# Four-unit stores, a longer scan ring and new queue orders in a fused scan and mixture-of-adapters kernel

## The chip, the core and the metric

The kernel runs on one core of a Trainium2 chip. The core has a matrix engine (PE, TensorE), a vector engine (DVE), a scalar engine (ACT), GpSimd (POOL) and a sync engine (SP). Sixteen DMA engines move data between the chip's main memory (HBM) and the core's on-chip memory; a queue of a sequencer (here mostly SP's) hands them their work. PE writes its results to eight banks of PSUM, from where ACT or DVE copy them out.

The metric is the device time of one execution in microseconds, lower is better: 201.49 us, the median of four runs (201.17 to 202.0).

## What is computed

A linear recurrence along the sequence, then a mixture of eight rank-16 adapters with the best two of eight experts for each row. Cut from the reference:

```python
# a, b: (8, 6400, 128) float32
for t in range(S):
    h = a[:, t] * h + b[:, t]
    out[:, t] = h

x = out.reshape(51200, 128)
logits = x @ w_gate                      # (51200, 8)
topk = the two largest of each row
w = softmax over the two chosen logits
delta = sum over both of  w * ((x @ A[e]) @ B[e])     # A: (8, 128, 16), B: (8, 16, 128)
return x + delta
```

26.2 MB each of a and b are read and 26.2 MB are written.

## The kernel before

**Units.** The 51,200 rows are cut into 100 units of 512 rows. A unit is one PSUM bank wide once transposed: 128 features on the partitions, 512 time steps along the row.

**The stages of a unit w**, with the names that the planner gives them:

- `lda`, `ldb` (function `load`): SP loads two units of a and two of b at a time, 512 KB each, in rows of 4 KB (one partition's share). They land in rings `a_in` and `b_in` of 8 slots, so 16 units deep (`ring`). The first a, the first two b and the last a are loaded alone, 256 KB in rows of 2 KB.
- `AB` (`transposes`): PE transposes a and b into two PSUM banks.
- `aev` (`a_evac`, L686): ACT copies the transposed a to `a_st`.
- `scan` (L710): DVE runs the recurrence and writes `xT`, a ring of `XR` = 20 units in f16.
- `ZL` (`products`): PE multiplies blocks of `xT` by the gate and all adapters' A side by side; `zl` (L767) parks the result on the chip, ACT again.
- gating (`m1`, `p1`, `r1`, `p3`, `m2`, `p4`, `r2`, `p6`, `p7`, `sig`): for groups of up to three units, on DVE, POOL and ACT. Groups among the first or last few (`quick`) take a shorter way through a MAX8 instruction on DVE.
- `mul` (L926): POOL, or DVE for some, multiplies by the gates. `T` transposes on PE, `tev` (L942) copies the result to `zwT` on DVE or ACT.
- `D` (`delta`): PE adds x (by the identity) and the product with B in a PSUM bank; `oev` (L978) copies it to `outt`, a ring of `NOUT` = 24 units.
- `st` (`store`): SP stores two units at a time, 512 KB.

**Which rows of x a partition holds.** A store wants long rows in memory. `x_block(v, q)` therefore picks columns of `xT` with a stride: for a pair of units (p, i) is split with i = 8, so that a partition gets 8 neighbouring rows of 128 floats, 4 KB, over the two units' places in `outt`. A unit that stands alone (`SOLO`) has i = 4, rows of 2 KB. Since a pair's rows are mixed over both units, products and deltas of a unit wait for the scan of the pair's last unit (`scanned`).

**Order.** Nothing is dispatched at run time: `_Plan.schedule` simulates all engines once, when the program is built, with the costs written in the code (a load of two units 1290 ns, and so on), and fixes each engine's list. Among operations that could start at the same time the one with the smaller key (unit plus the offset of its kind in `CFG["key"]`) goes first. `_Plan.run` (L243) then writes out each list; before an instruction it waits for the semaphores of what it needs (L248), and what follows on that engine waits too.

**Stores.** Store j of units from u0 has the rank u0 + `HOLD` among SP's work and waits for the evictions of its units and for the scan of unit u0 + `HOLD` (at most 99). `oev` of unit v waits for the store that last read its place, that of v - 24. All loads and stores are issued by SP in one list, by the line L429 of the helper `add_dma`; the three constants (w_gate, A, B) by ACT with the same helper at the start. A reaches `spread` (L533) on POOL and DVE, a gather on PE, and then the weights for `ZL`.

```python
        stores = [(u, 2) for u in range(0, NU - 2, 2)] + [(NU - 2, 1), (NU - 1, 1)]
...
                [f"oev{v}" for v in range(u0, u0 + n)] + [f"scan{min(u0 + HOLD, NU - 1)}"],
```

Of the kernel before, what the change touches and what calls it, by code (L numbers as in the profile page):

```python
# [11 lines left out]

CFG = {
    "ring": 8,
    "xr": 20,
    "zr": 48,
    "nout": 24,
    "hold": 20,
    "heads": (1, 1, 1, 1),
    "group": 3,  # L20
    "tails": (2, 2, 1, 1),
    "quick": (2, 2),
    "split": (4, 4),
    "solo": (2, 2),
    "mul": (0, 1, 0, 8),
    "tev": (1, 1, 4, 4),
    "tail": 8,
    "heat": 6,
    "filler": (2, 1, 1),
    "caps": {'a': 3, 'b': 4, 'Z': 1, 'O': 3, 'w': 8},  # L30
    "least": {'Z': 1, 'O': 1},
    "pairs": (98, 2),
    "ast": 3,
    "tevns": (264.0, 330.0),
    "key": {
        "AB": 170.4, "aev": 138.5, "scan": 13.3, "ZL": 157.0, "zl": 152.0, "gate": 31.6, "r1": -64.5, "r2": -65.8,
        "sig": 83.8, "mul": 73.7, "T": 119.3, "tev": 143.8, "D": 171.1, "oev": 151.4, "R": 65.1,
    },
}

# [239 lines left out]
def bass_associative_scan_2x2__then__mixture_of_adapters_kernel(  # L280
# [8 lines left out]
    NB, S, D = a.shape  # L289
    E = moe_w_gate.shape[1]  # L290
    R = moe_A.shape[2]
# [4 lines left out]
    Q = 4  # L296
    UT = 64 * QI
    assert UT == 128 * Q and N % (2 * UT) == 0 and S >= UT
    NU = N // UT
    RING = CFG["ring"]  # L300
    XR = CFG["xr"]
    NOUT = CFG["nout"]
# [33 lines left out]
    GB = GM * Q  # L336
    SOLO = [v for v in range(NU) if v < CFG["solo"][0] or v >= NU - CFG["solo"][1]]
    assert CFG["solo"][0] % 2 == 0 and CFG["solo"][1] % 2 == 0 and XR % 2 == 0 and NOUT % 2 == 0
    p0, p1 = CFG["pairs"]
    PAIRED = {w: (w - p0) % 2 for w in range(p0, NU - p1)}  # L340
    assert (NU - p0 - p1) % 2 == 0 and p0 >= 2 and p1 >= 1
# [15 lines left out]
    fills_of = {}  # L357
# [11 lines left out]
    with ExitStack() as stack:  # L369
# [4 lines left out]
        cst_f = sb(nc.sbuf_tensor("cst_f", [128, E + 256], F32))  # L374
# [14 lines left out]
        xT = sb(nc.sbuf_tensor("xT", [128, XR * UT], F16))  # L389
# [30 lines left out]
        def add_dma(name, eng, unit, starts, slot, ns, deps=(), kind="dma", issue=450.0, after=2000.0):  # L420
# [30 lines left out]
            ["id0"],  # L451
        )

        add_dma("wg_in", "act", -110, [(cst_f[:, 0:E], moe_w_gate[:, :])], ("wg",), 80.0, (), "fix", 450.0, 2000.0)
        add_dma(
            "A_in",
            "act",
            -109,
            [(cst_f[:, E : E + 128], moe_A.rearrange("e (h l) r -> (e h) (l r)", l=8))],
            ("A",),  # L460
            220.0,
# [4 lines left out]
        )  # L466
        add_dma(
            "B_in",
            "act",
            -108,  # L470
            [(cst_f[:, E + 128 : E + 256], moe_B.rearrange("e r d -> (e r) d"))],
            ("B",),
            220.0,
# [138 lines left out]
        def load(t, w):  # L612

            n = place(t, w)[0]
            many = 1 if (t, w) in alone else 2
            dst, i = rings[t][:, n % RING, :], QI
            if many == 1:
                dst, i = dst[:, column(t, w) : column(t, w) + UT], Q
            src = rows_of[t][w * UT : (w + many) * UT, :].rearrange("(p i) d -> p (i d)", i=i)
            for k in range(many):  # L620
                load_of[t, w + k] = f"ld{t}{w}"
            add_dma(
                f"ld{t}{w}",
                "sp",
                w - 2 * RING + (0 if w > 3 else -200),
                [(dst, src)],
                (t, n % RING, many, w if many == 1 else 0),
                1290.0 if many == 2 else 690.0,
                users.get((t, n - RING), []),
            )  # L630

        def transposes(w):
# [56 lines left out]
            )  # L689

        def readers(v):
            both = [v] if v in SOLO else [v - v % 2, v | 1]
            return [f"D{u}" for u in both] + [f"ZL{k}" for u in both for k in fills_of.get(u, [])]

        def scan(w):
            t0 = w * UT
# [33 lines left out]


        def x_block(v, q):
            if v in SOLO:
                x0 = (v % XR) * UT
                return xT[:, x0 : x0 + UT].rearrange("d (p i) -> d i p", i=Q)[:, q, :]
            x0 = (v - v % 2) % XR * UT
            return xT[:, x0 : x0 + 2 * UT].rearrange("d (p i) -> d i p", i=2 * Q)[:, v % 2 * Q + q, :]

        def scanned(v):
            return f"scan{v if v in SOLO else v | 1}"  # L740

        def products(k):
            b0, n = fills[k]
# [245 lines left out]
                gives=("O", v),  # L989
            )  # L990

        stores = [(u, 2) for u in range(0, NU - 2, 2)] + [(NU - 2, 1), (NU - 1, 1)]
        store_of = {v: j for j, (u0, n) in enumerate(stores) for v in range(u0, u0 + n)}

        def store(j):
            u0, n = stores[j]
            s0 = u0 % NOUT
            rows = out[u0 * UT : (u0 + n) * UT, :]
            tile, ns = outt[:, s0 : s0 + n, :], 680.0 * n
            if u0 in SOLO:  # L1000
                rows = rows.rearrange("(n p i) d -> p n (i d)", p=128, i=Q)
            else:
                rows = rows.rearrange("(p i) d -> p (i d)", p=128)
                tile, ns = tile.rearrange("p n c -> p (n c)"), 1290.0
            add_dma(
                f"st{j}",
                "sp",
                u0 + HOLD,
                [(rows, tile)],
                ("o", s0, n),  # L1010
                ns,
                [f"oev{v}" for v in range(u0, u0 + n)] + [f"scan{min(u0 + HOLD, NU - 1)}"],
            )

# [19 lines left out]
            gating(k)  # L1034
        for j in range(len(stores)):
            store(j)
        ends = [f"st{j}" for j in range(len(stores) - NOUT, len(stores))]
        add("end", "sp", "fix", 1.0e9, 10.0, lambda h: h.nop(), ends)

        plan.schedule()  # L1040
# [49 lines left out]
```

## Time and profile before

| | |
|---|---|
| median of four runs | 201.49 us (201.17 to 202.0) |
| the profiled execution | 201.28 us, of which the span from first to last instruction is 199.4 us |
| granted PE clock, mean | 0.984 |
| HBM read, written | 52.56 MB, 26.21 MB; 395 GB/s over the span |
| chain that ended last | PE 42%, DVE 20%, ACT 19%, DMA 6% |
| store of two units, issue to landing | 15.2 us (median of 49) |
| ACT copy to `a_st` | 100 copies, 61.6 us busy |
| ACT copy to `outt` | 100 copies, 61.3 us busy |
| DVE scan | 96 instructions of 128x512, 120.2 us busy |
| PE waiting for a_in or b_in | at most 2.0 us for each of the two in all |

The profile is one execution on the chip. Busy time is the union of an engine's instructions; consecutive instructions of one engine overlap, so that the mean length of one times their number is more than the busy time. PE is the matrix engine's multiplies, PEld its weight loads, which overlap them; matmuls are pipelined and their ends modelled, so a busy PE is not PE at its peak. "SPq" is SP's issuing of DMAs. A DMA queue's share is the time that its packets took, over sixteen DMA engines; packets of a queue overlap by a little, so a share can exceed 100%. A packet here is one row (2 or 4 KB) or one completion write. A line of stages reads: the window, its length, each engine's busy time and (xN) its instructions, then the granted PE clock, the DMA share and GB/s. A GB/s line has 40 equal slices of its window.

### The profile page before, as it was taken

The page shows a single profiled execution, that of the slowest core. Times are in us where ns is not written, and L with a number is a line of the kernel's source. Part 1 is how long each engine was busy: PE and PEld are TensorE (multiplying, and loading weights), DVE is VectorE, ACT ScalarE, POOL GpSimd, SP SyncE. Part 2 cuts the span into 40 slices and gives each one's busy share as a digit, 9 for nine tenths or more (in the row PEclk, how much of TensorE's full clock was granted, in tenths as well). Part 3 has the DMA queues.
Part 4 walks back from the last instruction along what each step waited for, and adds up shares of the span by engine and source line. Part 5 has one row for each costly group of instructions (what it writes and reads, how often), then busy time and mean ns, then how long its engine had stood idle before and what let it go on. Part 6 is the DMA issues. An engine that isn't in the chain of part 4 may idle for free.

```text
span 199.4 us, 8009 instructions
## 1 busy us (share of the span) xinstructions
PE 183.3 (92%) x3202; PEld 163.1 (82%) x3202; DVE 173.8 (87%) x302; ACT 179.9 (90%) x463; POOL 158.5 (80%) x278
## 2 busy tenths in 40 slices
PE   7887999999999999999999999999999999897750
PEld 4676898899999989899889998898899898795640
DVE  3799699999999999899989889889797999789940
ACT  3587899999999999999999999999999999898860
POOL 2344549889888998988799999998999989888710
PEclk9998799999999999999999999999999999999996
DMA  6999999999999999999999999999999999998993
GB/s 214 398 418 408 406 409 404 408 409 408 404 418 416 414 414 422 409 414 416 414 415 412 420 413 415 416 416 414 417 417 415 412 418 414 411 374 353 413 392 130
DMA packets 22629, 79.30 MB, mean 398 GB/s; under 512 B 2624, under 2 KB 2880, under 8 KB 22592
## 3 DMA queue, kind: packets, MB, share of 16 engines
q1 hardware_dynamic: 22160, 78.65, 98.0%
q8 instruction: 25, 0.41, 0.8%
q10 hardware_dynamic: 432, 0.14, 0.3%
q14 instruction: 12, 0.10, 0.1%
HBM read 52.56 MB, written 26.21 MB: 395 GB/s over the span
## 4 chain that ended last, share of the span: by engine, by line
PE 42%; DVE 20%; ACT 19%; DMA 6%; issue 3%; POOL 2%; SPq 2%; POOLq 1%; DVEq 0%; ACTq 0%
PE ps L94 22%; PE ps L98 20%; DVE xT L710 15%; ACT a_st L686 7%; DMA b_in<-in_b_dram 6%; ACT outt L978 5%; ACT zl L767 4%; DVE zwT L942 3%; SPq L429 2%; POOL zw L926 2%; ACT pn L816 1%; POOLq L369 1%; ACT g L905 1%; DVE zw L926 1%; POOL d L880 1%
## 5 line engine op out<-in xcount | busy, mean ns | idle before, releaser
L710 DVE TENSOR_TENSOR_SCAN xT<-a_st,xT,ps 128x512 f16<-128x512 f32 x96 | 120.2, 1252 | 10.9 <-ACT a_st L686 4.0
L926 POOL TENSOR_TENSOR zw<-zl,g 128x512 f16<-128x512 f32 x93 | 99.5, 1075 | 9.7 <-ACT g L905 8.0
L767 ACT COPY zl<-ps 128x408 f32<-128x408 f32 (+1 forms) x139 | 73.7, 537 | 1.0 <-PE ps L94 0.9
L98 PE MATMUL ps<-ident_f,a_in 64*128 64x64 f32 (+1 forms) x792 | 69.4, 231 | 1.2 <-DMA a_in<-in_a_dram 1.2
L98 PE MATMUL ps<-ident_f,b_in 64*128 64x64 f32 (+1 forms) x792 | 67.6, 230 | 1.5 <-DMA b_in<-in_b_dram 1.2
L686 ACT COPY a_st<-ps 128x512 f32<-128x512 f32 x100 | 61.6, 634 | 7.0 <-PE ps L98 6.4
L98 PEld LDWEIGHTS ps<-ident_f,a_in 64*128 64x128 f32 (+1 forms) x792 | 57.5, 140 | 8.7 <-DMA a_in<-in_a_dram 2.0
L978 ACT COPY outt<-ps 128x512 f32<-128x512 f32 x100 | 61.3, 629 | 2.2 <-PE ps L94 1.5
L98 PEld LDWEIGHTS ps<-ident_f,b_in 64*128 64x128 f32 (+1 forms) x792 | 56.5, 140 | 2.7 <-DVE m L851 1.3
L94 PE MATMUL ps<-cst_h,xT 128*128 128x136 f16 x400 | 50.7, 235 | 0.7 <-DVE xT L710 0.5
L94 PE MATMUL ps<-ident_h,xT 128*128 128x128 f16 x400 | 42.7, 229 | 1.4 <-DVE zwT L942 1.2
L98 PE MATMUL ps<-ident_h,zw 128*128 128x128 f16 x400 | 39.0, 220 | 3.7 <-DVE zw L926 2.0
L94 PEld LDWEIGHTS ps<-cst_h,xT 128*128 128x128 f16 x400 | 36.2, 148 | 4.7 <-DVE xT L710 1.4
L94 PE MATMUL ps<-cst_h,zwT 128*128 128x128 f16 x400 | 38.9, 220 | 0.0
L942 DVE COPY zwT<-ps 128x256 f32<-128x256 f32 x89 | 35.6, 408 | 2.6 <-PE ps L98 2.4
L94 PEld LDWEIGHTS ps<-ident_h,xT 128*128 128x128 f16 x400 | 33.1, 147 | 3.4 <-DVE zwT L942 2.4
L98 PEld LDWEIGHTS ps<-ident_h,zw 128*128 128x128 f16 x400 | 25.0, 98 | 7.8 <-DVE zw L926 3.0
L94 PEld LDWEIGHTS ps<-cst_h,zwT 128*128 128x128 f16 x400 | 27.4, 100 | 0.0
L816 ACT ACTIVATE pn<-d 128x96 f32<-128x96 f32 (+2 forms) x72 | 23.1, 329 | 0.8 <-POOL d L858 0.6
L866 POOL TENSOR_TENSOR L<-zl,pn 128x96 f32<-128x96 f32 (+2 forms) x34 | 13.0, 382 | 6.5 <-ACT pn L816 6.3
L888 POOL TENSOR_TENSOR d<-d 128x96 f32<-128x96 f32 (+2 forms) x36 | 13.9, 386 | 3.8 <-DVE d L841 3.3
L895 POOL TENSOR_TENSOR um<-d,pn 128x96 f32<-128x96 f32 (+2 forms) x36 | 14.3, 396 | 2.8 <-ACT pn L816 1.4
(38 smaller groups left out, 87.2 us busy)
## 6 DMA issues: line engine op xcount, KB each, us to landing
a_in<-in_a_dram SPq DMA_DIRECT2D x49, 512.0 KB, 15.4
b_in<-in_b_dram SPq DMA_DIRECT2D x49, 512.0 KB, 15.5
out_dram<-outt SPq DMA_DIRECT2D x49, 512.0 KB, 15.2
a_in<-in_a_dram SPq DMA_DIRECT2D x2, 256.0 KB, 8.9
b_in<-in_b_dram SPq DMA_DIRECT2D x2, 256.0 KB, 4.0
out_dram<-outt SPq DMA_DIRECT2D x2, 256.0 KB, 5.2
cst_f<-in_moe_A_dram ACTq DMA_DIRECT2D x1, 64.0 KB, 3.5
cst_f<-in_moe_B_dram ACTq DMA_DIRECT2D x1, 64.0 KB, 4.8
```

The costliest lines, as they stand in the source:

```text
L94: return self.handle.matmul(*args, **kwargs)
L98: return self.handle.transpose(*args, **kwargs)
L686: lambda h: h.copy(a_st[w % NAS][:, :], bank(("a", w))[:, :]),
L710: last = h.tensor_tensor_scan(out=x_at(lo, hi), data0=a_st[w % NAS][:, lo:hi], data1=bank(("b", w))[:, lo:hi], initial=init, op0=ALU.mult, ...
L767: return h.copy(zl[:, r0 : r0 + n, :], src)
L816: lambda h: h.activation(v(pn[s]), v(src[s]), ACTF.Relu, bias=bias, scale=scale),
L866: lambda h: h.tensor_tensor(out=v(L2[s]), in0=Lg, in1=v(pn[s]), op=ALU.subtract),
L888: lambda h: h.tensor_tensor(out=v(d1[s]), in0=v(d1[s]), in1=v(d2[s]), op=ALU.add),
L895: lambda h: h.tensor_tensor(out=v(um[s]), in0=v(d1[s]), in1=v(pn[s]), op=ALU.subtract),
L926: lambda h: h.tensor_tensor(out=oview, in0=zview, in1=gview, op=ALU.mult),
L942: return copy(zwT[v % NZT][:, :].bitcast(F32), bank(("O", v))[:, 0 : UT // 2])
L978: return copy(outt[:, v % NOUT, :], bank(("O", v))[:, :])
```

## The change

- Units 8 to 87 are stored four at a time, 1 MB in rows of 8 KB, the others in pairs but for the last two. `block_of` says which block a unit belongs to; `x_block`, `scanned`, `readers` and `stores` follow it. In a four-unit block the stride in `xT` is i = 16, and products and deltas wait for the scan of the block's last unit. The first two units, which stood alone, become a pair.
- The three constants are issued by POOL, A ahead of the rest.
- The `xT` ring holds 28 units rather than 20.
- A store waits for the scan 22 units on rather than 20.
- The sizes of the first and last gating groups, the number of quick groups, the split of products, the number of last units whose `mul` and `tev` may go to either of two engines, the units whose `tev` is on DVE (seven of eight rather than all between the ends), the warming multiplies at the start, the planner's costs of a load's latency and of stores, and the keys are set anew. The lists of all engines differ.
- The program's end waits for all stores rather than the last 24 of them; what that instruction waits for lies at the end of SP's list.

```diff
 CFG = {
     "ring": 8,
-    "xr": 20,
+    "xr": 28,
     "zr": 48,
     "nout": 24,
-    "hold": 20,
-    "heads": (1, 1, 1, 1),
+    "hold": 22,
+    "quads": (8, 12),
+    "heads": (1, 2, 1),
     "group": 3,
-    "tails": (2, 2, 1, 1),
-    "quick": (2, 2),
-    "split": (4, 4),
-    "solo": (2, 2),
-    "mul": (0, 1, 0, 8),
-    "tev": (1, 1, 4, 4),
-    "tail": 8,
+    "tails": (3, 2, 2),
+    "quick": (4, 2),
+    "split": (4, 8),
+    "solo": (0, 2),
+    "mul": (0, 1, 0, 10),
+    "tev": (7, 8, 4, 4),
+    "tail": 6,
     "heat": 6,
-    "filler": (2, 1, 1),
+    "filler": (2, 2, 2),
...
     "key": {
-        "AB": 170.4, "aev": 138.5, "scan": 13.3, "ZL": 157.0, "zl": 152.0, "gate": 31.6, "r1": -64.5, "r2": -65.8,
-        "sig": 83.8, "mul": 73.7, "T": 119.3, "tev": 143.8, "D": 171.1, "oev": 151.4, "R": 65.1,
+        "AB": 26.2, "aev": 28.9, "scan": 8.5, "ZL": -146.0, "zl": 94.8, "gate": -12.7, "r1": 84.9, "r2": 34.5,
+        "sig": 37.7, "mul": 31.8, "T": -42.2, "tev": 33.0, "D": 9.7, "oev": 472.4, "R": 65.09967571861861,
     },
...
+    QUAD = range(CFG["quads"][0], NU - CFG["quads"][1])
+    assert not QUAD or (XR % 4 == 0 and NOUT % 4 == 0 and QUAD[0] % 4 == 0 and len(QUAD) % 4 == 0)
+
+    def block_of(v):
+
+        n = 1 if v in SOLO else 4 if v in QUAD else 2
+        return v - v % n, n
+
...
-        add_dma("wg_in", "act", -110, [(cst_f[:, 0:E], moe_w_gate[:, :])], ("wg",), 80.0, (), "fix", 450.0, 2000.0)
+        add_dma("wg_in", "pool", -107.4, [(cst_f[:, 0:E], moe_w_gate[:, :])], ("wg",), 80.0, (), "fix", 450.0, 2000.0)
         add_dma(
             "A_in",
-            "act",
-            -109,
+            "pool",
+            -107.5,
...
         add_dma(
             "B_in",
-            "act",
-            -108,
+            "pool",
+            -107.3,
...
+                after=2000.0 if many == 2 else 1250.0,
...
         def readers(v):
-            both = [v] if v in SOLO else [v - v % 2, v | 1]
-            return [f"D{u}" for u in both] + [f"ZL{k}" for u in both for k in fills_of.get(u, [])]
+            if v < 0:
+                return []
+            u0, n = block_of(v)
+            whole = range(u0, u0 + n)
+            return [f"D{u}" for u in whole] + [f"ZL{k}" for u in whole for k in fills_of.get(u, [])]
...
         def x_block(v, q):
-            if v in SOLO:
-                x0 = (v % XR) * UT
-                return xT[:, x0 : x0 + UT].rearrange("d (p i) -> d i p", i=Q)[:, q, :]
-            x0 = (v - v % 2) % XR * UT
-            return xT[:, x0 : x0 + 2 * UT].rearrange("d (p i) -> d i p", i=2 * Q)[:, v % 2 * Q + q, :]
+            u0, n = block_of(v)
+            x0 = u0 % XR * UT
+            return xT[:, x0 : x0 + n * UT].rearrange("d (p i) -> d i p", i=n * Q)[:, (v - u0) * Q + q, :]
 
         def scanned(v):
-            return f"scan{v if v in SOLO else v | 1}"
+            u0, n = block_of(v)
+            return f"scan{u0 + n - 1}"
...
-        stores = [(u, 2) for u in range(0, NU - 2, 2)] + [(NU - 2, 1), (NU - 1, 1)]
+        stores = []
+        for v in range(NU):
+            u0, n = block_of(v)
+            if v == u0:
+                stores += [(v, n)]
...
-            rows = out[u0 * UT : (u0 + n) * UT, :]
-            tile, ns = outt[:, s0 : s0 + n, :], 680.0 * n
-            if u0 in SOLO:
-                rows = rows.rearrange("(n p i) d -> p n (i d)", p=128, i=Q)
-            else:
-                rows = rows.rearrange("(p i) d -> p (i d)", p=128)
-                tile, ns = tile.rearrange("p n c -> p (n c)"), 1290.0
             add_dma(
                 f"st{j}",
                 "sp",
                 u0 + HOLD,
-                [(rows, tile)],
+                [
+                    (
+                        out[u0 * UT : (u0 + n) * UT, :].rearrange("(p i) d -> p (i d)", p=128),
+                        outt[:, s0 : s0 + n, :].rearrange("p n c -> p (n c)"),
+                    )
+                ],
                 ("o", s0, n),
-                ns,
+                {1: 690.0, 2: 1290.0, 4: 2510.0}[n],
                 [f"oev{v}" for v in range(u0, u0 + n)] + [f"scan{min(u0 + HOLD, NU - 1)}"],
             )
...
-        ends = [f"st{j}" for j in range(len(stores) - NOUT, len(stores))]
+        ends = [f"st{j}" for j in range(len(stores))]
```

## The prediction

> **What bounds the kernel now.** I read the page first, for the engines against the DMA queues.
>
> ```profile
> span 199.4 us, 8009 instructions
> PE 183.3 (92%) x3202; PEld 163.1 (82%) x3202; DVE 173.8 (87%) x302; ACT 179.9 (90%) x463; POOL 158.5 (80%) x278
> DMA  6999999999999999999999999999999999998993
> q1 hardware_dynamic: 22160, 78.65, 98.0%
> a_in<-in_a_dram SPq DMA_DIRECT2D x49, 512.0 KB, 15.4
> ```
>
> No compute engine is full over the span, though ACT and PE come near. SP's queue q1 fills 98.0% of sixteen DMA engines' span, and a 512 KB load needs 15.4 us from issue to landing, so some twelve transfers stand in line at any time. The bytes are fixed by the problem; only the cost per byte and the two ends can give.
>
> Next, whether compute could go faster if it were let: the stages, for ACT's copies of the decay (a_st, one per unit) and for the output evictions (outt).
>
> ```profile
> 20.00:40.00 20.00, 8.75 (x15) 0.94 1.03 407
> 40.00:60.00 20.00, 7.75 (x13) 1.00 1.03 410
> 60.00:80.00 20.00, 6.40 (x12) 1.00 1.03 416
> ...
> 40.00:60.00 20.00, 7.24 (x11) 1.00 1.03 410
> ```
>
> From 40 to 60 us ACT took in 13 units (above) and put out 11 (last line): 12 units in 20 us, 1.67 us each. The DMA engines move 768 KB a unit, at 415 GB/s (100 to 150 us) some 1.9 us. Compute has about 0.25 us a unit in hand although its engines look full.
>
> Then the end, DMA and work in the last microseconds.
>
> ```profile
> GB/s 179 384 384 410 384 435 384 410 410 333 384 410 410 384 384 371 410 295 64 51 51 51 51 51 51 38 38 26 26 26 26 26 26 13 0 0 0 0 0 0
> q1 hardware_dynamic: 476, 1.18, 47.0%
> ...
> L429 SPq DMA_DIRECT2D out_dram<-outt x10: 332/662/1189, 181.9 to 193.8; - x10
> DMA to landing us min/median/max: 5.1/7.0/8.1
> ...
> 180.21 1.27 DVE L710 TENSOR_TENSOR_SCAN xT<-a_st,xT,ps 128x512 f16<-128x512 f32 x1
> 191.22 2.38 ACT L978 COPY outt<-ps 128x512 f32<-128x512 f32 x4 [0.71 <-PE ps L94]
> ```
>
> The first lines cover 193 to 199.4 us in slices of 0.16 us. At 196 us the rate falls from 384 to 51 and later to 26 GB/s, and 415/16 is 26: two engines, then one, still drain a queue. The last eviction ends at 191.22 + 2.38 = 193.6, the last store is issued at 193.8 and lands 5.1 us later, at 198.9. So the slowest DMA engine ends the span. A 4 KB load on an idle queue landed in 3.0 us; with 0.7 us for 256 KB the last store needs about 3.7 us alone. Compute therefore has 5.1 - 3.7 = 1.4 us in hand at the end.
>
> **The change, part by part.** *8 KB rows.* Two windows give the price of a row:
>
> ```profile
> q1 hardware_dynamic: 5666, 20.64, 101.7%
> ...
> q10 hardware_dynamic: 432, 0.14, 10.7%
> ```
>
> 100 to 150 us: 1.017 x 16 x 50 = 813.6 us of engine time for 5038 rows of 4 KB and 628 completion writes. A completion write costs between 0 and 8.56/432 = 20 ns (the constants' queue, 2 to 7 us); I take 10, and a 4 KB row is 160.2 ns. 193 to 199.4 us: 48.1 us for 416 rows in 1.18 MB, so 160 of 4 KB and 256 of 2 KB, and 60 completions: a 2 KB row is 85.5 ns. The part that does not grow with bytes is 2 x 85.5 - 160.2 = 10.8 ns. Twenty stores of four units replace forty of two. Per engine that is 8 x 10.8 ns of rows and one completion of 10 ns less for each: 20 x 96 ns = 1.9 us. The first store goes from 2 KB to 4 KB rows: 16 x 85.5 - 8 x 160.2 = 0.09 us. Together 2.0 us. Low end: the engine cuts an 8 KB row in two, and 0.3 us is left. Below nothing: the only packets over 4 KB in the trace are instruction fetches, 25 of 16 KB with 0.8% of 16 x 199.4 us, 1.02 us each beside other traffic. A row at half of that, 510 ns, would cost 160 x 190 ns = 30 us more. I take 2.0, since the two sizes on the same queue are nearest.
>
> The Trainium skill speaks for less: "DMA: Bandwidth & Descriptors", section "Why small descriptors are slow (HBM only)", gives about 3 cycles a packet, and section "Where 436 GB/s comes from" a fabric of 850 MHz. By my estimate that is 3.5 ns a row, 0.6 us in all, and a time of 200.7; the 10.8 ns of the rows above stands against it.
>
> *Strided weights.* Rows of a four-unit block make PE read xT at a stride of 32 bytes for the 8 weight loads of each of 80 units; pairs have 16 bytes, single units 8. Loads last 113 ns for single units, 146 for pairs, 98 when contiguous. They overlap; a group of four multiplies takes 0.39 us for a single unit and 0.42 for a pair. Doubling the stride again costs between 0 and twice that step, 0.06 us a group or 0.12 us a unit, which lies in the 0.25 us in hand. I take 0. Without cover it would be 80 x 0.12 = 10 us.
>
> The Trainium skill, "SBUF — State Buffer", section "Door 1: The DMA port swizzle (why `[64,N]` ≈ `[32,N]`)", has lines of 16 bytes and a penalty for each access that enters a new one. By that a pair's stride pays the whole penalty already (the step from 113 to 146 ns agrees) and 32 bytes add nothing.
>
> *Constants on POOL.* Three issues leave ACT (0.41 to 0.45 us each) and stand on POOL: A's ahead of the identity's select, the other two ahead of the spread. POOL's price is not in the trace; I bound it by ACT's 0.45 and by the first load issue that had to wait, 2.06 us, and take the nearer 0.45. The identity is ready at 1.7 or 3.3 us, first needed at 3.6. The spread starts at 4.8 as now, or at 0.93 + 3 x 2.06 + 0.3 = 7.4, 2.6 us late, and behind it wait the gather and all later transposes on PE. Loads issued near 9 us land 15 us later, so the DMA queue hides this up to about 10 us. Zero; with the cover gone, 2.6. ACT's earlier table load (2.1 us) gains nothing, its first copy waits for PE until 4.8.
>
> *Orders.* The first store moves back past two loads on SP, and each store needs four evictions and a scan 22 units on, not 20. Evictions stand at most 19 units behind the input copies in both orders, so the store is not asked earlier than its data. Behind a waiting store are the loads, and behind them PE's transposes; the queue's 12 to 15 us cover it. SP has 31 store issues for 51, at 0.4 to 1.1 us, all under that cover. The xT ring of 28 only relaxes scan's wait for readers. Nine zwT copies (0.36 us) move from VectorE to ACT: 3.2 us over 90 units, 0.04 each, inside the 0.25. Two more warming multiplies and 28 more MAX8 (0.09 us) lie at the ends, under the queue.
>
> *Sum.* Compute's end follows the DMA: 2.0 us gained. Compute's end stays: 1.4 us. I take 1.7: 201.28 - 1.7 = 199.6 (199.4 span and 1.9 around it, so a span of 197.7). The profiled run lies 0.2 under the median of 201.49, which leaves the forecast between 199.6 and 199.8.
>
> **Rivals.** *The row saving does not come.* For it: 4 KB rows already move 415 GB/s. Against: the 85.5 and 160.2 ns. 201.28 - 0.3 = 201.0.
>
> *The drain ends it, slower than before.* After the last input copy, ACT now has 15 evictions to do, before 12; PE 13 and 15 groups of transposes and deltas after its last input transpose, before 9 and 11. The drain ran from the last scan's end, 181.5, to 193.6: 1.0 us an eviction. Three more put the last at 196.6, and 3.7 us for the store at 200.3 instead of 198.9: 202.7. For it: the counts. Against: work left for later makes the last scan earlier, since one PE does both. It decides slower from a last eviction at 195.8 on.
>
> *Longer reads or rows cost.* Weight loads uncovered, or rows priced like fetches: a tenth of the 30 us above gives 201.28 + 3 - 0.3 = 204. Against: pairs cost 6 to 8 ns a load over single units.
>
> *The slowest engine falls back less.* It trails by some 2.5 us at the end (196 to 198.5). One instruction fetch of 1.0 us fewer on it gives 198.6.
>
> **How the numbers follow.** Forecast 0.60, its own range 198.9 to 200.5; slowest engine better 0.04; no row saving 0.12; drain 0.18; longer reads or rows 0.06. About 0.3%, 0.6 us, is what can be told from no change here. Faster 0.64, same 0.12, slower 0.24. The range takes in the first three cases but the low tail, and the nearer half of the drain: 198.6 to 202.6.
>
> **What would show it.** DMA share still 0.9 and more from slice 2 to the tail; q1 with 51 - 31 = 20 x 16 fewer completions and 2,560 + 128 fewer rows, 22160 - 3,008 = 19,152; the packet count at 8 KB and over up by 2,560. Engine time of a long row near 310 ns: right; 320: the first rival. Weight loads of xT still near 146 ns: right. Last eviction before 193, last store landing over 3.7 us after issue: the DMA still ends it. A last eviction past 195.8 or a DMA share under 0.9 before 175 us makes the prediction wrong, and so would PE waiting for a_in or b_in after 20 us.

## The result, and the profile after

| | before | after |
|---|---|---|
| median | 201.63 us (64 runs, 201.03 to 202.47) | 201.91 us (43 runs, 201.02 to 203.48) |
| ratio of the times | | 1.0015, 95% interval 1.0005 to 1.0024 |
| the profiled execution, span | 201.28, 199.4 us | 201.60, 199.8 us |

The change costs 0.3 us (0.1 to 0.5) where 1.7 were to be gained. 

The page of the changed kernel, in the order used before: span, engines, DMA share in 40 slices, queues, issues.

```profile
span 199.8 us, 7937 instructions
PE 187.1 (94%) x3204; PEld 164.9 (83%) x3204; DVE 171.0 (86%) x313; ACT 180.5 (90%) x467; POOL 158.3 (79%) x269
...
DMA  5999999999999999999999999999999999979985
GB/s 174 340 418 408 411 404 403 411 407 408 409 412 414 419 420 411 423 414 413 414 421 415 420 412 417 416 416 420 417 417 422 410 414 422 424 330 399 387 355 206
...
q1 hardware_dynamic: 19152, 78.65, 97.3%
...
q0 software_dynamic: 96, 0.14, 0.3%
...
a_in<-in_a_dram SPq DMA_DIRECT2D x49, 512.0 KB, 17.2
...
out_dram<-outt SPq DMA_DIRECT2D x20, 1024.0 KB, 17.9
```

q1 has the 19,152 packets that were counted and the same bytes. Its share fell from 98.0% to 97.3% although the span is longer: the queue's work did shrink. The losses are at the two ends. The second slice of GB/s has 340 (398 before), and near the end the DMA row has a 7 and an 8 (175 to 180 and 190 to 195 us), where the row of before has 9 both times. The GB/s row of before:

```profile
GB/s 214 398 418 408 406 409 404 408 409 408 404 418 416 414 414 422 409 414 416 414 415 412 420 413 415 416 416 414 417 417 415 412 418 414 411 374 353 413 392 130
```

The steady stretch, 100 to 150 us, q1 alone (before: 5666 packets, 20.64 MB, 101.7%):

```profile
q1 hardware_dynamic: 4716, 20.72, 101.1%
```

The engines spend 0.6% less time and move 0.4% more. In the packet records an 8 KB row takes 309 ns (median), a 4 KB row 159: the forecast looked for 310.

The weight loads of `xT` (products and deltas; ns min, median, max), then those of before from 100 to 150 us:

```profile
L95 PEld LDWEIGHTS ps<-cst_h,xT x400: 112/145/177, 13.2 to 186.6; 128*128 128x128 f16 x134
L95 PEld LDWEIGHTS ps<-ident_h,xT x400: 112/148/175, 22.2 to 194.7; 128*128 128x128 f16 x134
```

```profile
L94 PEld LDWEIGHTS ps<-cst_h,xT x123: 141/145/171, 100.1 to 148.5; 128*128 128x128 f16 x123
L94 PEld LDWEIGHTS ps<-ident_h,xT x120: 142/146/168, 100.3 to 149.5; 128*128 128x128 f16 x120
```

Twice the stride costs nothing that can be seen here (145 and 148 ns against 145 and 146).

The end: ACT's last evictions (start and length), all evictions, the issues of stores, and the time from issue to landing:

```profile
192.66 1.07 ACT L990 COPY outt<-ps 128x512 f32<-128x512 f32 x2 [0.17 <-PE ps L95]
...
194.58 1.24 ACT L990 COPY outt<-ps 128x512 f32<-128x512 f32 x2
```

```profile
L990 ACT COPY outt<-ps x100: 568/656/820, 23.9 to 195.2; 128x512 f32<-128x512 f32 x100
L438 SPq DMA_DIRECT2D out_dram<-outt x31: 332/461/4092, 46.2 to 195.8; - x31
...
DMA to landing us min/median/max: 3.4/15.1/20.1
```

The last eviction ends at 195.8 us instead of 193.6, and the last store needs 3.4 us instead of 5.1: it finds nearly empty queues. The slowest DMA engine still has a line: its last landings come 1.27 to 1.36 us apart for each 512 KB, up to the last. So computation and slowest engine end together in this execution.

The head, that is, the first microseconds: POOL's instructions (start, length, and in brackets the idle time before, with its releaser), then stages of 2 us (each engine's busy time, the granted PE clock, the DMA share, GB/s), and last the first two stages of before.

```profile
1.30 0.70 POOL L438 DMA_DIRECT2D cst_f<-in_moe_A_dram  x1 [0.36 <-POOL ident_f L444]
2.10 0.30 POOL L451 TENSOR_SCALAR_AFFINE_SELECT ident_f<-ident_f 128x128 f32<-128x128 f32 x1
2.34 0.56 POOL L438 DMA_DIRECT2D cst_f<-in_moe_w_gate_dram  x1
2.90 0.71 POOL L438 DMA_DIRECT2D cst_f<-in_moe_B_dram  x1
6.20 1.47 POOL L542 TENSOR_TENSOR spread<-cst_f,mine 128x384 f16<-128x384 f32 x1 [2.59 <-DMA cst_f<-in_moe_A_dram]
```

```profile
4.00:6.00 2.00, 1.50 (x10) 1.00 (x8) 0.00 (x0) 0.59 (x1) 0.00 (x0) 1.00 0.79 261
6.00:8.00 2.00, 0.19 (x3) 0.22 (x4) 1.85 (x2) 0.00 (x0) 1.66 (x2) 0.93 1.00 317
8.00:10.00 2.00, 2.00 (x17) 1.69 (x16) 0.10 (x1) 0.36 (x2) 0.29 (x1) 0.50 1.02 391
10.00:12.00 2.00, 2.00 (x12) 1.10 (x13) 0.95 (x1) 0.49 (x1) 0.00 (x0) 0.50 1.03 422
12.00:14.00 2.00, 2.00 (x22) 1.16 (x18) 0.76 (x2) 0.59 (x1) 0.00 (x0) 0.50 1.03 422
```

```profile
4.00:6.00 2.00, 1.94 (x10) 1.35 (x8) 1.25 (x2) 0.59 (x1) 1.20 (x1) 1.00 1.04 382
6.00:8.00 2.00, 1.67 (x21) 1.46 (x22) 0.77 (x1) 0.82 (x2) 0.56 (x2) 1.00 1.00 399
```

A's issue took 0.70 us on POOL (0.45 had been taken) and its data landed 4.7 us after the issue began (3.5 before). PE had nothing to do for 2.3 us until the gather at 7.8 us; then its granted clock stood at 0.50 until past 14 us, and the loads ran at 261 and 317 GB/s from 4 to 8 us (382 and 399 before).

### The profile page after: what moved, and what is told of

It is laid out like the page before. It is cut to its first block, busy times and chain, and to the rows that moved or that the text cites. A ratio compares the mean times of both kernels' runs of the same rounds, so it can differ in the third digit from the quotient of the medians.

```text
span 199.8 us, 7937 instructions
## 1 busy us (share of the span) xinstructions
PE 187.1 (94%) x3204; PEld 164.9 (83%) x3204; DVE 171.0 (86%) x313; ACT 180.5 (90%) x467; POOL 158.3 (79%) x269
## 3 DMA queue, kind: packets, MB, share of 16 engines
q1 hardware_dynamic: 19152, 78.65, 97.3%
## 4 chain that ended last, share of the span: by engine, by line
PE 51%; ACT 22%; DVE 16%; issue 3%; DMA 2%; POOL 1%; POOLq 1%; DVEq 0%; ACTq 0%
PE ps L99 26%; PE ps L95 26%; DVE xT L723 11%; ACT a_st L696 9%; ACT outt L990 5%; ACT zl L779 5%; DMA cst_f<-in_moe_A_dram 2%; DVE zwT L954 2%; DVE zw L938 2%; ACT pn L828 1%; ACT zwT L954 1%; POOLq L378 1%; POOL spread L542 1%; ACT g L917 1%; DVE um L907 1%
## 5 line engine op out<-in xcount | busy, mean ns | idle before, releaser
L696 ACT COPY a_st<-ps 128x512 f32<-128x512 f32 x100 | 62.7, 660 | 6.9 <-PE ps L99 6.3
L99 PE MATMUL ps<-ident_f,b_in 64*128 64x64 f32 (+1 forms) x792 | 66.7, 230 | 0.6 <-DVE xT L723 0.5
L990 ACT COPY outt<-ps 128x512 f32<-128x512 f32 x100 | 64.3, 666 | 1.1 <-PE ps L95 0.7
L95 PE MATMUL ps<-cst_h,xT 128*128 128x136 f16 x400 | 51.5, 237 | 0.8 <-DVE xT L723 0.6
L99 PE MATMUL ps<-ident_h,zw 128*128 128x128 f16 x400 | 37.8, 219 | 2.0 <-POOL zw L938 1.4
L954 DVE COPY zwT<-ps 128x256 f32<-128x256 f32 x80 | 32.1, 408 | 1.8 <-PE ps L99 1.7
L907 POOL TENSOR_TENSOR um<-d,pn 128x96 f32<-128x96 f32 (+1 forms) x31 | 12.2, 395 | 2.4 <-ACT pn L828 1.7
L900 POOL TENSOR_TENSOR d<-d 128x96 f32<-128x96 f32 (+2 forms) x33 | 13.3, 402 | 0.5
L878 POOL TENSOR_TENSOR L<-zl,pn 128x96 f32<-128x96 f32 (+1 forms) x30 | 12.3, 409 | 1.7 <-ACT pn L828 1.7
```

Source lines behind the costliest of these rows:

```text
L95: return self.handle.matmul(*args, **kwargs)
L99: return self.handle.transpose(*args, **kwargs)
L696: lambda h: h.copy(a_st[w % NAS][:, :], bank(("a", w))[:, :]),
L878: lambda h: h.tensor_tensor(out=v(L2[s]), in0=Lg, in1=v(pn[s]), op=ALU.subtract),
L900: lambda h: h.tensor_tensor(out=v(d1[s]), in0=v(d1[s]), in1=v(d2[s]), op=ALU.add),
L907: lambda h: h.tensor_tensor(out=v(um[s]), in0=v(d1[s]), in1=v(pn[s]), op=ALU.subtract),
```

## The experiments

The ratios are to the kernel before, run beside each on the same chip, with 95% intervals; in microseconds they are taken times 201.5. A ratio is worked out over all runs of a set, so it need not be the quotient of the medians. "Before" and "after" are the two kernels; the short names f1 to f7 stand for the transfers alone, below.

### The parts of the change in the kernel itself

**Constants back on ACT.** The three constants go to the front of ACT's list after the planner is done; every other list stays.

```diff
+        consts = [plan.ops[n] for n in ("wg_in", "A_in", "B_in")]
+        for op in consts:
+            plan.order["pool"].remove(op)
+        plan.order["act"][:0] = consts
```

> The changed kernel with its three constants issued by ACT again; every list stays as it was but for those three. Theory head: the constants on POOL hold up the slowest DMA engine by 1.5 us in the first 15 us and that delay is carried to the end, so the fifth 512 KB load of a lands near 14.6 us, not 16.1, and the time is 0.5 to 1.5 us under the changed kernel's, a ratio to before of 0.994 to 0.999. Rival drain: the last eviction at 195.8 us sets the end whatever the DMA does, so the loads land earlier and the time stays, ratio 1.001.

201.22 us, ratio 0.9976 (0.9957 to 0.9995): a little quicker than before, and by the ratios than after (1.0015). The same kernel once more later, as a control:

> The control: the constants on ACT's queue ahead of the table load, as in the first run. 201.1 to 201.4 us, last eviction 193.5, by both readings.

201.52 us, 0.9992 (0.9973 to 1.0011). Its profiled executions are told apart below.

**Before, with its constants on POOL** in the places that the change gives them.

```diff
+        wg_in, a_in_, b_in_ = [plan.ops[n] for n in ("wg_in", "A_in", "B_in")]
...
+        at = plan.order["pool"].index(plan.ops["id"])
+        plan.order["pool"][at : at + 1] = [a_in_, plan.ops["id"], wg_in, b_in_]
```

> The kernel before with its three constants issued by POOL, A ahead of the identity's select, in the places of the changed kernel; nothing else moves. Theory head: 1.5 us more, ratio 1.0075, with loads from the third on landing 1.5 us later. Rival (the queue hides the head, as predicted): ratio 1.000.

202.13 us, 1.0018 (0.9996 to 1.0040). A landed 5.4 us after its issue, and the last eviction ended at 195.9 us.

**Long rows cut in half.** After, each store of four units as two DMAs of 512 KB with 4 KB rows, in the same place; then the same with the constants on ACT.

```diff
+            cuts = 2 if n == 4 else 1
+            w = n * UT // cuts
...
+                [(to[:, c * w : (c + 1) * w], tile[:, c * w : (c + 1) * w]) for c in range(cuts)],
```

> The changed kernel with each four-unit store issued as two of 512 KB with rows of 4 KB, at the same place of SP's list; all lists otherwise equal. Theory rows: an 8 KB row saves about 10 ns, so the last load lands 14 x 0.08 = 1.1 us later, near 176.4 us, and the time rises by 1.1 to 1.6 us, ratio 1.007 to 1.009. Rival (a row of 8 KB costs as two of 4 KB): last load at 175.3 us, ratio 1.0015.

> The changed kernel with its constants issued by ACT and each four-unit store cut into two of 4 KB rows; all lists otherwise equal to the changed kernel's. Beside the run with constants on ACT alone it prices the long rows without POOL's scatter. Theory rows, as predicted: 1.6 to 1.9 us over that run, ratio to before 1.005 to 1.007. Theory overlap (successive rows overlap, so that only some 0.04 us a store is saved): 0.5 to 0.9 us over it, ratio 1.000 to 1.002. Rival (rows save nothing): ratio 0.998.

202.46 us, 1.0041 (1.0020 to 1.0062), and 202.27 us, 1.0028 (1.0009 to 1.0046). The second is the new lists, ring and four-unit blocks without long rows and without POOL's issues: 0.56 us slower than before. Against it, long rows gain 0.52% with the first run of the constants on ACT and 0.36% with the control; with the constants on POOL, 0.26% by after's own ratio. That is 1.05, 0.7 and 0.5 us, each with about half a microsecond to either side. The half rows differ from those of before in one thing: they lie 8 KB apart in memory, not end to end. In the steady stretch, 100 to 150 us, that shows no cost: 5666 packets, 20.63 MB and 101.6% (below), where before had 5666, 20.64 and 101.7%.

Where the gain goes is seen in the steady stretch, q1 from 100 to 150 us, half rows first, then long rows, both with the constants on ACT:

```profile
q1 hardware_dynamic: 5666, 20.63, 101.6%
```

```profile
q1 hardware_dynamic: 4719, 20.69, 101.1%
```

Engine time for a megabyte falls by 0.8% (101.6/20.63 to 101.1/20.69), but only 0.3% more is moved. The rest fits a smaller overlap: rows overlapped by 1.6% of the engines' time, now by 1.1%. A price worked out from durations counts that part as gain.

**Four-unit stores on the lists of before.** The code of after with ring, hold, group sizes and keys of before, constants on ACT, `quads` alone added; the first two units are stored singly.

> The kernel before with four-unit stores for units 8 to 87 and nothing else of the change: its constants on ACT, its ring of 20, its keys; the planner orders anew, and the first two units are stored one by one. Theory rows plus head: the row saving of 1.1 to 1.6 us is seen undisturbed, ratio 0.992 to 0.995. Rival (four-unit blocks make evictions and scans later and the DMA engines run dry): ratio 1.000 or more, with the DMA share under 0.9 before 175 us or the last eviction past 195 us.

204.57 us, 1.0119 (1.0081 to 1.0158). The last eviction ended at 199.1 us and the DMA row of its page ends in 9175. On the old ring, keys and group sizes the blocks cost more (some 2.4 us) than long rows gain. So they need other lists; whether there are lists for them that cost nothing was not tried.

### The transfers alone

These kernels compute nothing. They issue all loads and stores on SP in about the kernel's order; the second (f2) differs from the first (f1) by the lengths of the stores, the third (f3) from the second by the queue of the constants.

```diff
-    QUADS, CONST = False, 'act'
+    QUADS, CONST = True, 'act'
```

> The transfers alone: all loads of a and b and all stores in the order of loads and two-unit stores, the constants on ACT, no computation (the outputs are zeros). Theory: the DMA engines are the bound of the whole kernel, so this stays within 4 us of the kernel before; its time is the base for the next two.

> The same transfers alone with four-unit stores for units 8 to 87 (outputs zeros). Theory rows, as predicted: 1.9 us under the run with pairs. Theory overlap: 0.5 to 1.0 us under it. Rival (rows save nothing): equal within 0.2 us.

> The transfers alone with four-unit stores and the constants issued by POOL (outputs zeros). Theory head: 0.7 to 1.5 us over the same with constants on ACT, the first 512 KB loads landing up to 2 us later. Rival (it was PE waiting for the late constants, not the DMA): equal within 0.2 us.

195.81, 196.52 (four runs, 195.56 to 197.13) and 195.94 us. The kernel before is 5.7 us above its own transfers, although its DMA engines look almost as full. No gain of long rows is seen here, and the constants on POOL come out 0.58 us lower, not higher, both within the scatter of four runs. What is missing was looked for in the queue that these kernels do not have at all, q8: PE's instructions, fetched in 25 blocks of 16 KB by the same sixteen engines. 3,200 matmuls on a constant tile, which nothing waits for, bring them back in f4, f5 and f6, the same three otherwise.

```diff
+        @block.tensor
+        def _(h):
+            h.wait_ge(warm, 1)
+            for n in range(3200):
+                last = h.matmul(ps[:, 0:128], warm_t[:, :], warm_t[:, :])
+            last.then_inc(heat, 1)
```

> The transfers alone with stores of two (195.8 us), plus 3,200 matmuls on a constant tile that nothing else waits for; they stand in for PE's instruction stream, which the engine must fetch from memory in blocks of 16 KB (25 in the kernels). All computation is left out, the output is zeros. Theory (each fetch sets the one DMA engine that carries it back by 1.0 to 1.4 us, and the engine that got most of them ends the span): about 25 fetches, some engines with two or three; the spread between the first and the last engine's landing of one load grows to 3 us or more; time 195.8 + 2 to 4 = 198 to 200 us. Rival (the five and a half us above the transfers alone come from waits of the computation): 195.6 to 196.4, the fetched 0.4 MB being 0.5% of the bytes, spread over sixteen engines.

> The same with stores of four units for units 8 to 87. All computation is left out. Theory (an engine that is late by its fetches keeps its own line of rows, so long rows gain what they gain on that engine): 0.5 to 1.0 us below the kernel with stores of two and the same matmuls. Rival (drift of the engines eats it, as without matmuls): within 0.5 us of it, or above.

> The same again with the three constants loaded by GpSimd. All computation is left out. Theory that the disturbed head comes back on the engine that ends the span: 0.4 to 0.9 us above the kernel with the constants loaded by ACT and the same matmuls. Rival (the head's delay costs only where the computation waits for it): within 0.3 us.

199.91, 199.08 and 199.51 us (0.9918, 0.9882 and 0.9898, each with some 0.0014 to either side). The control, f7, does the same multiplying in 800 matmuls of 512 columns:

> The transfers alone with stores of two, plus 800 matmuls of 512 columns on the constant tile: PE does the same multiplying as with 3,200 of 128 columns, in a quarter of the instructions. All computation is left out, the output is zeros. Theory (the fetches of PE's instructions cost it): about 6 fetches instead of 25, so that few engines get one or two; 196.3 to 197.5 us. Rival (PE's work itself, its power or its reading, slows the transfers): 199 to 200 us, as with 3,200.

196.08 us, below the range expected. f1, f4 and f7 ran on three chips; by their ratios to the kernel before (0.9710, 0.9918 and 0.9722) the steps are 4.2 and 0.2 us, which agrees. The queues of f1, f4 and f7 (packets, MB, share of the engines):

```profile
q1 hardware_dynamic: 21600, 78.65, 100.0%
```

```profile
q1 hardware_dynamic: 21600, 78.65, 98.2%
q8 instruction: 25, 0.41, 0.8%
```

```profile
q1 hardware_dynamic: 21600, 78.65, 99.8%
...
q8 instruction: 6, 0.10, 0.2%
```

25 fetches of 1.0 us are 0.8% of the sixteen engines' time, 1.6 us if they were shared evenly; they cost 4.1. Six cost 0.3. The landings of one load near 121 us on the sixteen engines (sorted, us after the first engine) say why:

```
f1   0.0 0.0 0.0 0.0 0.1 0.1 0.1 0.1 0.2 0.2 0.2 0.3 0.3 0.3 0.4 1.4
f4   0.0 0.1 0.2 0.2 0.2 0.4 0.6 3.1 3.1 3.2 3.3 3.3 3.4 3.5 3.7 5.0
f7   0.0 0.0 0.0 0.0 0.1 0.1 0.1 0.1 0.1 0.2 0.3 1.3 1.4 1.6 1.7 1.7
```

In f7 five engines are one step late; in f4 eight are two steps behind the best and one three. The steps follow the fetches. The packet records of f7 have fetches at these times, and the landings of the next load shown have so many engines more than 1 us late:

| f7: last fetch before, us | none | 21.2 | 48.8 | 76.3 | 92.0 (8 KB, q14) | 104.1 | 131.6 | 159.4 |
|---|---|---|---|---|---|---|---|---|
| load landing from, us | 20.0 | 22.5 | 50.7 | 79.4 | 94.4 | 105.6 | 131.8 | 161.8 |
| engines late | 0 | 1 | 2 | 3 | 4 | 5 | 6 | 7 |

The single late engine of f1 comes the same way, after its only fetch in the span (8 KB in q14, at 90.9 us). At 20.0 us no engine of f7 is more than 0.4 us behind the first; the late ones stand 1.5 to 1.8 us behind it (after the 8 KB fetch 1.1). So a fetch sets one engine back, and nothing evens it out: the largest lag is 1.7 to 1.9 us all the way from 22.5 to 161.8 us. The time is that of the engine set back most. In f7 each late engine is one step behind, as the single one of f1 is, so f7 takes hardly longer.

With the fetches in place long rows gain 0.83 us (f5 against f4) and the constants on POOL cost 0.43 (f6 against f5), both with some 0.4 us to either side. By this the kernel before is 1.5 us above its transfers, not 5.7. Its twelve fetches of 8 KB in q14, of which f4 has one, may be part of what remains; they were not added.

### What the constants on POOL cost

The first profiles suggested the computation: late A, idle PE, half the clock. The end of a unit's scan and of its eviction (us, from the timelines) show how such a delay is carried. "ACT, A late" is a version that follows below the table:

| unit | before | before, constants on POOL | after, constants on ACT | after | ACT, A late |
|---|---|---|---|---|---|
| 4 | 14.1 / 34.8 | 18.4 / 36.8 | 14.6 / 31.9 | 18.4 / 34.3 | 20.5 / 36.3 |
| 24 | 45.4 / 72.4 | 47.7 / 74.7 | 47.0 / 76.7 | 49.5 / 78.9 | 51.5 / 81.2 |
| 60 | 105.6 / 133.5 | 107.9 / 135.8 | 109.8 / 136.3 | 112.1 / 138.6 | 114.3 / 140.8 |
| 99 | 181.5 / 193.6 | 183.8 / 195.9 | 179.0 / 193.5 | 181.3 / 195.8 | 183.4 / 197.9 |

In both pairs 2.2 to 2.5 us at unit 24 are 2.3 us at unit 99: from there on nothing is made up. At unit 4 the scans are further apart (4.3 and 3.8 us); there the quicker kernels still had a half clock before them, for 3.4 us from 18.9 us in before and from 17.0 with the constants on ACT, while after had its 6.8 us from 7.7 on. So the half clock is not the change's alone. ACT alone, from 140 to 170 us of after, shows an engine with nothing in hand:

```profile
140.00:160.00 20.00, 19.98 (x54) 1.00 1.02 417
160.00:170.00 10.00, 10.00 (x28) 1.00 1.02 417
```

Whether this costs time was tested from both sides: after once more; after with nine more warming multiplies ahead of the gather, so that PE keeps its clock; and the constants on ACT, but A last and behind the table load. In the expectations reading 1 is that the first loads are disturbed, reading 2 that the computation is late.

```diff
-                for _ in range(CFG["filler"][w]):
+                for _ in range(CFG["filler"][w] + (9 if w == 0 else 0)):
```

```diff
-        plan.order["act"][:0] = consts
+        plan.order["act"][:0] = [consts[0], consts[2]]
+        spot = plan.order["act"].index(plan.ops["table"]) + 1
+        plan.order["act"].insert(spot, consts[1])
```

> The changed kernel once more, on the chip of the three runs beside it. If the idle stretch of PE before the gather and the fall of its granted clock to 0.50 belong to this kernel, they come again, with a last eviction near 195.8 us and 201.9 us; if they were one execution's, the last eviction is near 193.9 as in the run with half rows, and the time 201.4 to 202.5.

> The changed kernel with nine more warming multiplies (some 1.9 us) ahead of the gather, so that PE is busy while A is on its way through GpSimd's queue; all DMA issues and lists as in the changed kernel. Reading 2 (clock and computation): the clock stays near 1.00 from 8 to 14 us, the computation is late by 1.2 us or less instead of 2.3, last eviction 193.6 to 194.8, time 201.2 to 201.6. Reading 1 (rows of the first loads): 201.9, within 0.2 of the changed kernel, whatever the last eviction does.

> The version with the constants on ACT's queue, but with A issued after the table load, some 2.5 us later, and w_gate and B before it. GpSimd issues nothing and the first loads are undisturbed. Reading 2: A lands at 6.5 to 7.5 us, PE idles 2 us or more, the clock falls to 0.50, last eviction 195.5 to 196.5, time 201.7 to 202.3. Reading 1: the loads are on time, so 201.2, within 0.2 of the control.

After again: 201.82 us, 0.9992 (0.9973 to 1.0012); clock kept: 201.68, 0.9988 (0.9969 to 1.0006); A late: 201.67, 0.9997 (0.9976 to 1.0018). None can be told from another, nor from the control's 0.9992, so this set has no difference between after and the constants on ACT that could be explained. Reading 2 wanted the clock kept to be 0.3 to 0.7 us quicker than after, and A late slower than the control; both differences are 0.1 us, as reading 1 had it, but with 0.4 us to either side, and the 201.2 us that reading 1 gave for A late did not come. In the second profile of after, A landed 4.1 us after its issue, PE's clock held, and the last eviction ended at 193.0; that execution took 201.41 us, not the 198.8 that 2.8 us less would make. The slowest DMA engine ended it, 6.0 us after the last issue. So the late computation of the first profile was that execution's, and without it the time was nearly the same (201.41 against 201.60). With A late (issued at 1.7 us, the last of the three, landed 6.4 us later) the clock did fall, from 10 to 16 us:

```profile
10.00:12.00 2.00, 2.00 (x17) 1.69 (x17) 0.21 (x1) 0.27 (x1) 0.14 (x1) 0.50 1.02 416
...
14.00:16.00 2.00, 2.00 (x20) 1.20 (x18) 0.76 (x2) 0.59 (x1) 0.00 (x0) 0.50 1.05 424
```

```profile
L438 SPq DMA_DIRECT2D out_dram<-outt x31: 332/344/4142, 48.2 to 197.9; - x31
...
DMA to landing us min/median/max: 2.4/13.1/20.7
```

Its last store landed 2.4 us after its issue at 197.9, on idle queues, and the execution took 202.70 us: there the drain did end it. So the computation decides from a last eviction somewhere between 195.8, where both end together, and 197.9.

Reading 1, the loads: moved by 20 us were 7.20 MB in the profile of before and in the first with the constants on ACT (201.28, 201.30 us), 6.92 in the control (202.00), 6.72 in after, 6.96 in its second profile. Stages of the first run with constants on ACT, then of its control, the same kernel (last two columns: DMA share, GB/s):

```profile
4.00:6.00 2.00, 2.00 (x9) 1.41 (x8) 0.94 (x2) 0.59 (x1) 1.06 (x1) 1.00 1.05 408
6.00:8.00 2.00, 2.00 (x19) 1.29 (x18) 1.11 (x1) 0.32 (x2) 0.79 (x3) 1.00 1.01 395
```

```profile
4.00:6.00 2.00, 2.00 (x10) 1.54 (x9) 1.02 (x2) 0.59 (x1) 1.26 (x1) 1.00 0.93 330
6.00:8.00 2.00, 2.00 (x19) 1.46 (x18) 1.02 (x1) 0.27 (x1) 0.64 (x3) 1.00 0.87 336
```

The 0.28 MB between them are 0.67 us at 415 GB/s, and the two times are 0.70 us apart. Other executions do not follow this: after with its clock kept had moved 6.73 MB by 20 us, as after, and took 202.36 us, against 201.60. To see whether such a head belongs to the new lists, the kernel before was profiled twice more.

> The kernel before, once more. Theory (the slow stretch of the first loads comes by chance in any kernel and sets the time): a profile of 201.2 to 201.5 us goes with 380 GB/s or more from 4 to 8 us, one of 201.9 or more with 350 or less. Rival (it is the new lists that slow the first loads): 380 or more whatever the time.

> As the run beside it, a third profile of the kernel before, with the same two expectations.

201.64 and 201.56 us. Stages of the first:

```profile
4.00:6.00 2.00, 2.00 (x10) 1.55 (x9) 1.10 (x2) 0.59 (x1) 1.29 (x2) 1.00 1.00 341
6.00:8.00 2.00, 0.64 (x6) 0.27 (x5) 0.95 (x1) 0.00 (x0) 0.30 (x2) 1.00 0.99 318
```

Both have the slow head (6.97 and 6.98 MB by 20 us), so it is not the lists that make it; but these executions were quicker than the theory's 201.9. The profile of before that the forecast started from had a better head than the two later ones.

What POOL's issues add is small beside this scatter. Five comparisons give it: after against constants on ACT, first runs 0.39% and second runs 0.00%; the two kernels with half rows 0.13%; the kernel before 0.18%; the transfers with fetches 0.43 us. The mean is 0.4 us, each with about half a microsecond to either side. A sixth, f3 against f2, has 0.58 us the other way; with it the mean is 0.2. So that POOL's issues cost time is likely, not shown, and the way is open: f6 has it without any computation, which speaks for the loads.

## Why the prediction was wrong

It held that the slowest DMA engine ends the span, that the queue's work shrinks by 2.0 us, and that all else costs nothing. The step that failed is the second, and after it the two zeros of the third. The first is right: it ends the profiles of before, of after (level with the drain) and of all variants but three: before with its constants on POOL and the version with A late, where that engine's landings have gaps, and the four-unit stores on the old lists. The sum is not:

| step | forecast, us | runs, us |
|---|---|---|
| "8 KB rows … Together 2.0 us" | -2.0 | -0.8 (-1.05, -0.83, -0.7, -0.5) |
| "Orders … all under that cover" | 0 | +0.56 (+0.2 to +0.9) |
| "Constants on POOL … Zero" | 0 | +0.4 (0 to +0.8) |
| sum | -1.7 with compute's limit | +0.2, against the measured +0.3 |

The sum comes near by construction, since most of these prices lead step by step from before to after; it does not test the single terms. Each has an uncertainty of some half a microsecond, so that only the sign of the first two is clear.

- **"8 KB rows", "Together 2.0 us": the mechanism is right, the size is not.** Rows cost what was read from the windows (309 ns where 310 was foretold), but the step took 96 ns from durations for each store. By the shares above 100%, rows overlap, and more so the shorter they are, so that more than half of the saving had been hidden already; that explanation fits the shares and was not tested by itself. The range's low end, "the engine cuts an 8 KB row in two", was the wrong bound for that; the shares over 100% that the prediction quoted were the sign. Its estimate of 0.6 us beside the sum was nearer than the 2.0 taken. And the 25 fetches of 16 KB were not the only packets over 4 KB before: q14 has twelve of 8 KB, 309 ns in the median, so the duration of a long row could have been read there.

- **"Constants on POOL", "Zero".** POOL's issue was priced at 0.45 us and measured 0.56 to 0.71; what comes later in the head is A's landing, 3.8 to 5.4 us after issue against 3.3 to 3.6 from the front of ACT's list (4.3 and 4.4 against 4.0 to 4.2 in the transfers alone). The step counted on loads that land 15 us later to hide it. They can hide PE's wait, but not slower first loads; that these are what costs the 0.4 us is not shown. The Trainium skill, "DMA: Bandwidth & Descriptors", section "SWDGE vs HWDGE vs iDMA", says that descriptors for GpSimd's DMAs are computed by software and that the other path sets up faster; the landing times agree.

- **"Orders", cost zero.** With half rows and constants on ACT the new lists are 0.56 us slower. In that profile the last store is issued at 193.6 us, about as before (193.8), and lands 6.2 us later, not 5.1; the two later profiles of before have 5.7 and 6.3 with issues at 193.6 and 192.9. So it lies with the DMA engines again, at the ends and not in the steady stretch, where the two are equal; why they end later was not settled.

- **"Compute has about 0.25 us a unit in hand"** came from 20 us in which ACT took in 13 units and put out 11. The table of units speaks against it: nothing is made up over 75 units, and ACT is busy for practically all of 140 to 170 us. "Compute's end stays: 1.4 us" was fair for a computation on time; a late head spends it, as in the first profile of after, where the last store landed 3.4 us after issue, under the 3.7 that was to show the DMA as the bound.

- **The rivals.** "The drain ends it" named the right threshold, 195.8 us, where after's profile lies; what brought it there was not the count of evictions at the end (with constants on ACT the same lists end at 193.5, and in after's second profile at 193.0) but a late head. "The row saving does not come" is nearest in time (201.0) and half right. "The slowest engine falls back less" was given 0.04 and one fetch of 1.0 us; fetches are the largest term above the transfers, 4.1 us in the kernels without computation.

- **Right:** 19,152 packets; a long row of 309 ns; weight loads of 145 and 148 ns; DMA share of 0.9 and more from the second slice up to 175 us.

The lowest of the versions is the changed kernel with its constants on ACT: 0.9976 (0.9957 to 0.9995) and 0.9992 (0.9973 to 1.0011) of before in two sets of runs, 0.2 to 0.5 us. Only the first set's interval leaves 1 out, and in the second set after has the same 0.9992.

## What to carry to other kernels

Where sixteen DMA engines each carry their own share of every transfer, as the landings here show, the time is that of the engine with the most extra work, so build the kernel's transfers alone, add what else uses those engines, and read the floor from that before pricing rows. A saving worked out from durations that overlap (a share above 100%) must be measured before it is counted on; here less than half of it came. A statically ordered computation whose engines are full can carry a late start to its last instruction (2.3 us over 75 units here), so what is issued ahead of the first transfers deserves a price of its own, and one profile of a head says little: this one came in two forms in the same kernel.

## What the runs showed of the hardware

- **Instruction fetches.** 25 blocks of 16 KB, half a percent of the bytes, take the transfers from 195.81 to 199.91 us; six blocks, with the same PE work, to 196.08. Each leaves one engine some 1.5 us behind the others. The Trainium skill, "Runtime: NRT & Kernel Launch", section "Instruction fetch mechanics", has blocks of 16 KB and 256 instructions, which agrees (6,400 instructions, 25 blocks), and calls the cost of crossing a block mostly hidden. For PE, which runs them, it was (idle for 1.0 us in f4, at the start alone); for a kernel bound by its transfers it was not. Fewer and wider matmuls in the kernel itself were not tried.
- **Long rows without fetches showed no gain:** 196.52 us (195.56 to 197.13) against 195.81, and in the profiled execution (197.13 us) landings up to 3.6 us apart between engines (0.3 to 1.6 with 4 KB rows).
- **The clock.** PE was idle for 2.3 us before the gather and granted 0.50 for the next 6.8 us in one execution of after, and not in another, where A came 0.6 us sooner and PE was idle for 1.5 us. The idle time alone does not decide it: in the control the clock fell for 3.4 us at 17.4 us, with no idle stretch over 0.6 us in the 8 us before.
- **The software queue** put the constants' 0.14 MB in 96 packets, where ACT's queue makes 432.
